# Split probabilities for the third block of the first batch, roundings on ScalarE alone, and a planner that holds DMAs back

## The chip, the cores and the metric

The kernel runs on one core of a Trainium2 chip. The metric is device microseconds of one execution. Times are compared between kernels run on the same chip.

## The reference

Two batches of 8 heads (768 tokens, head size 64) go through an attention whose mask joins only tokens with equal hash buckets; the result, as 1536 tokens of 512, goes through two gated layers of width 2048.

```python
def _attn_ref(q, k, v, proj):
    q_bits = (np.einsum('bhsd,dk->bhsk', q, proj) > 0).astype(np.int64)   # 6 hash bits, k likewise
    ...
    mask = q_bucket[:, :, :, None] == k_bucket[:, :, None, :]
    scores = scale * np.matmul(q, k.transpose(0, 1, 3, 2))
    scores = np.where(mask, scores, -1000000000.0)
    scores = scores - np.max(scores, axis=-1, keepdims=True)
    attn = np.exp(scores)
    attn = attn / (np.sum(attn, axis=-1, keepdims=True) + 1e-09)
    return np.matmul(attn, v)

def _moe_ref(x, w_in, w_out):        # _moe2_ref: g = h * clip(h + 3, 0, 6) / 6
    h = x @ w_in
    g = h * (1.0 / (1.0 + np.exp(-h)))
    return g @ w_out
```

The four weight matrices arrive as 64-bit floats, all else as 32-bit.

## The kernel before

**Stages.** A matrix product of nearly fp32 precision is made of three fp16 products: each operand is a high part (its rounding to fp16) and a low part (the rest). The work is, in program order: the preparation of four head pairs of batch 0 (load q and k, scale, split into high and low parts, transpose by DMA, hash, transpose again), their attention, the first layer of batch 0 (`mlp1`), the same for batch 1, then the second layer of both batches (`mlp2`).

**Attention.** A `Unit` is one head pair and one block of two query tiles; it has four slots (two tiles by two heads). Batch 0 has 4 pairs by 3 blocks, so 12 units and 48 slots, as has batch 1. A slot is: four score matmuls (L755, L756), a row maximum on VectorE (L759), two tiny steps (L761, L764), the exponential `e` on ScalarE (L767), and the product with v. That product comes in two kinds. An exact slot (`exact_values`) turns the fp32 `e` on TensorE (L783, six transposes), copies the result out of PSUM in two halves (L789), and multiplies in fp32 (L795, six matmuls that the trace shows as twelve). A split slot (`split_values`) rounds `e` to a high part `PN` (L814 on ScalarE or L815 on VectorE), subtracts for the low part (L816 on GpSimd or L817 on VectorE), has both turned by one DMA on SP's queue (L819), and multiplies in fp16 with the split `V` (L809, 18 matmuls). In the kernel before, all 48 slots of batch 0 are exact (`NX = 12`) and read v as it was loaded; all of batch 1 are split.

**Weights.** W1I and W1O are the two matrices of the first layer, in 16 chunks each. A chunk is loaded into one of three staging buffers `st` (L450); ScalarE or GpSimd makes a copy (L452, L453), GpSimd clears part of `st` (L455), and VectorE puts the bits together in two steps (L457, L459), the second of which frees the buffer. The scales come out of sums over all chunks of a matrix: W1O's scale needs all 16 of its chunks. Then each of the 32 pieces is split into a high and a low part. The first product of `mlp1` (L882) needs W1I; the second (L939, destination `h` from `G`) needs W1O. The second layer's matrices go the same way later.

**split().** The helper makes a high part on GpSimd (L392) or on ScalarE (L393), and a low part on VectorE (L400) from the source and the high part. It splits weights, the gated activations `G` of `mlp1`, `V` of batch 1, and q and k of each pair. Of q (i = 0) it uses another form (L385 to L390): GpSimd scales in place, ScalarE copies, GpSimd or VectorE subtracts.

**What sets the order.** No order is written out. `Plan` records every step with its engine, or with several engines to choose from, a cost in us, and what it reads and writes. `Run` then walks through the steps as a list scheduler: it takes at each point the step that can start first, ties by rank, and chooses among engines by the earlier end. VectorE steps marked `True` and all of GpSimd's are kept from running at the same time (`port`). 24 passes, forward and backward in turn, improve the ranks; the forward run with the shortest modelled length is kept, and the instructions of all engines are issued in its order. Each engine, and SP's queue of DMAs, then runs its instructions strictly in that order and waits where an operand isn't there.

## Time and profile before

| | |
|---|---|
| median of three runs | 773.67 us (772.26 to 777.58) |
| the profiled execution's own time | 777.89 us |
| its span in the trace | 776.2 us |
| instructions in the trace | 15453 |
| TensorE busy | 717.7 us (92%) |
| VectorE busy | 519.3 us (67%) |
| ScalarE busy | 460.1 us (59%) |
| GpSimd busy | 256.2 us (33%) |
| mean granted TensorE clock | 0.978 |

The span runs from the first to the last instruction; the execution's own time has 1.7 us around it. A share of busy time is a mean over stages with different limits, so the stretches are read apart. In the rows, PE is TensorE, PEld its weight loads, DVE VectorE, ACT ScalarE, POOL GpSimd, SPq SP's queue of DMAs.

### The profile page before, as it was taken

How to read it: one execution, taken by the hardware profiler on the slowest of the kernel's cores; microseconds unless marked ns; L12 is line 12 of the kernel's file. 1: busy time of each engine (PE TensorE's matmuls, PEld its weight loads, DVE VectorE, ACT ScalarE, POOL GpSimd, SP SyncE). 2: the span in 40 equal slices, each digit the busy share in tenths (PEclk: the TensorE clock that was granted, in tenths of full speed). 3: DMA queues.
4: the chain of work that ended last, by engine and by line, in shares of the span. 5: the costliest groups of instructions: out<-in, count | busy, mean ns of one | idle time of the engine just before them, and what ended most of it. 6: DMA issues, size and time to landing. Idle time of an engine off the chain costs nothing.

```text
span 776.2 us, 15453 instructions
## 1 busy us (share of the span) xinstructions
PE 717.7 (92%) x6012; PEld 535.7 (69%) x6012; DVE 519.3 (67%) x1147; ACT 460.1 (59%) x941; POOL 256.2 (33%) x263
## 2 busy tenths in 40 slices
PE   1498999999768999999989999999999999999997
PEld 1287898988647888887878888984444664444564
DVE  5798799898993876689777685879433343333343
ACT  6497799987633758888754646546333434323433
POOL 3435232444554546667734353521000000000000
PEclk9998899999988999999999999999999999999999
DMA  9999535759465478699953536000000100000100
GB/s 283 251 254 216 173 111 174 159 139 224 137 126 103 90 126 162 146 177 169 185 167 110 190 109 214 5 1 1 1 1 0 55 1 28 1 1 0 55 1 28
DMA packets 157385, 84.89 MB, mean 109 GB/s; under 512 B 139904, under 2 KB 147072, under 8 KB 157312
## 3 DMA queue, kind: packets, MB, share of 16 engines
q1 hardware_dynamic: 157312, 83.91, 44.6%
q8 instruction: 47, 0.77, 0.4%
q14 instruction: 26, 0.21, 0.1%
HBM read 44.57 MB, written 3.15 MB: 61 GB/s over the span
## 4 chain that ended last, share of the span: by engine, by line
PE 67%; DVE 11%; DMA 7%; ACT 6%; issue 3%; POOL 2%; SPq 0%; POOLq 0%; ACTq 0%; DVEq 0%
PE h L882 27%; PE s L1027 16%; PE h L939 10%; PE o L795 5%; PE s L755 3%; PE s L756 2%; DVE w L400 2%; PE h L783 2%; DVE nm L759 2%; PE o L809 2%; DMA st<-in_moe_w_in_dram 2%; ACT e L767 2%; DMA PT<-PN 2%; DMA st<-in_moe_w_out_dram 1%; DMA T<-N 1%
## 5 line engine op out<-in xcount | busy, mean ns | idle before, releaser
L939 PE MATMUL h<-G,w 128*128 128x256 f16 x1152 | 137.3, 277 | 4.2 <-DVE w L400 4.2
L1027 PE MATMUL s<-y,G 128*128 128x512 f16 x576 | 134.4, 379 | 0.8 <-ACT w L1043 0.8
L939 PEld LDWEIGHTS <-w 128*128 128x128 f16 x1152 | 112.7, 100 | 21.0 <-DVE w L400 5.3
L882 PEld LDWEIGHTS <-w 128*128 128x128 f16 x1152 | 112.6, 99 | 18.0 <-DVE g L927 1.8
L759 DVE TENSOR_REDUCE nm<-s 128x1 f32<-128x768 f32 x96 | 91.1, 952 | 25.0 <-PE s L756 24.4
L767 ACT ACTIVATE e<-s,nb,sc 128x768 f32<-128x768 f32 x96 | 95.0, 991 | 20.3 <-DVE nb L764 16.6
L1014 ACT ACTIVATE g<-h,table 128x256 f32<-128x256 f32 x96 | 50.7, 562 | 83.4 <-PE h L882 83.3
L1027 PEld LDWEIGHTS <-G 128*128 128x128 f16 x576 | 56.3, 98 | 62.8 <-issue 1.1
L816 POOL TENSOR_TENSOR PN<-e,PN 128x768 f16<-128x768 f32 x48 | 80.4, 1679 | 37.6 <-ACT PN L814 28.0
L1018 DVE TENSOR_SCALAR g<-g 128x512 f32<-128x512 f32 (+1 forms) x64 | 23.5, 367 | 94.5 <-ACT g L1014 94.5
L882 PEld LDWEIGHTS <-T 128*128 128x128 f16 x576 | 56.3, 98 | 42.2
L795 PE MATMUL o<-w,PT 128*128 128x64 f32 x576 | 72.4, 278 | 1.4 <-DVE x L844 1.4
L455 POOL TENSOR_SCALAR st<-st 128x512 f32<-128x512 f32 x64 | 46.1, 724 | 82.8 <-ACT w L452 34.7
L795 PEld LDWEIGHTS o<-w,PT 128*128 128x128 f32 x576 | 70.9, 198 | 2.6 <-DVE x L844 1.9
L755 PE MATMUL s<-T 128*128 128x384 f16 x192 | 65.5, 341 | 7.4 <-ACT e L767 7.3
L1021 ACT ACTIVATE G<-g 128x512 f16<-128x512 f32 (+1 forms) x64 | 33.4, 522 | 61.1 <-DVE g L1020 59.5
L882 PE MATMUL h<-X,w 128*128 128x256 f16 x576 | 67.7, 272 | 0.9 <-DVE g L927 0.9
L756 PE MATMUL s<-T 128*128 128x384 f16 x192 | 65.6, 342 | 3.0 <-DMA T<-N 2.8
L882 PE MATMUL h<-T,w 128*128 128x256 f16 x576 | 65.8, 276 | 2.0 <-DVE g L927 2.0
L1022 DVE TENSOR_TENSOR G<-g,G 128x512 f16<-128x512 f32 (+1 forms) x64 | 35.7, 558 | 39.2 <-ACT G L1021 38.5
L392 POOL TENSOR_SCALAR G<-g,table 128x512 f16<-128x512 f32 x39 | 43.1, 1105 | 40.2 <-DVE g L927 34.1
L882 PE MATMUL h<-X,T 128*128 128x512 f16 (+1 forms) x288 | 50.7, 326 | 0.0
(136 smaller groups left out, 1159.9 us busy)
## 6 DMA issues: line engine op xcount, KB each, us to landing
st<-in_moe_w_in_dram SPq DMA_DIRECT2D x32, 512.0 KB, 4.3
st<-in_moe_w_out_dram SPq DMA_DIRECT2D x32, 512.0 KB, 4.0
qk<-in_v_dram SPq DMA_DIRECT2D x8, 384.0 KB, 3.7
out_dram<-w SPq DMA_DIRECT2D x12, 256.0 KB, 2.0
qk<-in_q_dram SPq DMA_DIRECT2D x6, 384.0 KB, 3.4
qk<-in_k_dram SPq DMA_DIRECT2D x6, 384.0 KB, 4.0
w<-in_v_dram SPq DMA_DIRECT2D x2, 768.0 KB, 9.6
T<-T SPq DMA_DIRECT2D x8, 192.0 KB, 3.6
```

Of the source, the lines that this page charges most:

```text
L392: op([(POOL, Cost.pool_ts(n), lambda: nc.gpsimd.tensor_scalar(hi(), src(), scale(), 1.0, op0=ALU.mult, op1=ALU.mult)), (ACT, Cost.act_ap(n ...
L455: op((POOL, Cost.pool_ts(512), lambda: nc.gpsimd.tensor_scalar(st.t[:, :, 1].bitcast(F32), st.t[:, :, 1].bitcast(F32), 0.0, 1.0, op0=ALU.m ...
L755: nc.tensor.matmul(o, t.t[:, 0, c, :], t.t[:, 1, ks, :], start=True, stop=False)
L756: nc.tensor.matmul(o, t.t[:, 2, c, :], t.t[:, 3, ks, :], start=False, stop=True)
L759: op((DVE, 0.865, lambda: nc.vector.tensor_reduce(nm.t, ps.t[:, :, :HS], op=ALU.max, axis=AX.XY, negate=True)), [(ps, 0)], [(nm, 0)])
L767: op((ACT, 0.97, lambda: nc.scalar.activation(e.t.rearrange("p (n c) -> p n c", n=2), ps.t[:, :, :HS], AF.Exp, bias=nb.t, scale=sc.t, accu ...
L795: nc.tensor.matmul(po(), pt.t[:, kt, :], vraw.t[:, v0 + a, kt * D : (kt + 1) * D], start=(kt == 0), stop=(kt == T - 1))
L816: op(ways((POOL, Cost.pool_tt(S), lambda: nc.gpsimd.tensor_tensor(pn.t[:, 1], e.t, pn.t[:, 0], op=ALU.subtract)), (DVE, Cost.tt(S), lambda ...
L882: nc.tensor.matmul(ph, W[f, wl, kt, :], XT[b].t[:, kt, ts, xl, :], start=(c == 0), stop=(c == 3 * NK - 1))
L939: nc.tensor.matmul(pf.t[:, :n], W1O[f, wl, slice(m * P, (m + 1) * P)], G.t[:, f, gl], start=(f == 0 and c == 0), stop=(f == NF - 1 and c = ...
L1014: nc.scalar.activation(g.t[:, cs], pf.t[:, cs], AF.Relu, bias=three, scale=a)
L1027: nc.tensor.matmul(acc[m // 2].t[:, m % 2, :DM], gs.t[:, f % 3, gl, m * P : (m + 1) * P], W2O[f, wl], start=(f == 0 and c == 0), stop=(f = ...
```

## The change

Three edits, one of which sits in the planner, so that nearly the whole order of instructions is another.

**Which slots are exact.** `exact(p, blk)` takes the place of `NX`: blocks 0 and 1 of batch 0 stay exact (32 slots), block 2 (16 slots) becomes split. So v of batch 0 is split as well, four pieces of 768 elements per partition.

**Roundings.** `split()` makes every high part on ScalarE; the choice of GpSimd and the in-place form for q are gone, and so is GpSimd's choice for the copy of a weight chunk. Over the program this takes 39 high parts of weights, 39 of `G`, 5 + 2 of q and k, 3 of `V` and 4 chunk copies from GpSimd, and for the eight q splits the scaling in place and the subtraction; VectorE gets eight low parts more for q and four for `V`. By the program's lists GpSimd goes from 268 to 179 instructions, ScalarE from 742 to 817, VectorE from 1149 to 1159, and SP from 202 to 218 (16 more transposes of `PN`).

**The planner.** In the forward and backward runs a step of SP starts no earlier than 2.0 us (`QUEUE`) before the modelled end of the transfers already issued. This holds in the planner alone: on the chip SP waits for nothing more than before. What changes is the place of a DMA in the order.

```diff
@@ -40,6 +40,7 @@
 
     DMA_ISSUE, DMA_START = (0.51, 1.22), (1.1, 1.27)
     TURN_END = 0.86
+    QUEUE = 2.0
 
     WINDOW, WARM = 10240 / 3000, 1.294
 
@@ -127,7 +128,7 @@
         self.last = [[-10.0] * 5 for _ in ops]
         self.free, self.held, self.port = [0.0] * 5, {}, 0.0
         self.order, self.engines, self.ends = [], [None] * n, [0.0] * n
-        data, clock = 0.0, Clock(always=back)
+        self.data, clock = 0.0, Clock(always=back)
         self.pending = [[] for _ in range(5)]
         for i in range(n):
             if not left[i]:
@@ -140,7 +141,7 @@
             way = next(w for w in self.ways[i] if w[0] == e)
             time = way[1]
             if e == SP:
-                end = data = max(s + Cost.DMA_START[o.turn], data) + time
+                end = self.data = max(s + Cost.DMA_START[o.turn], self.data) + time
                 self.free[e] = max(s + Cost.DMA_ISSUE[o.turn], o.turn * (end - Cost.TURN_END))
             elif e == PE:
                 end = self.free[e] = clock.run(s, time)
@@ -171,6 +172,9 @@
         r = self.free[e]
         if e == POOL or e == DVE and shared(next(w for w in self.ways[i] if w[0] == e)):
             r = max(r, self.port)
+        if e == SP:
+
+            r = max(r, self.data - Cost.QUEUE)
         if self.take[i] is not None:
             held = self.held.get(self.take[i], 0.0)
             if held is None:
@@ -379,19 +383,9 @@
 
         op((ACT, Cost.act(n) + 0.093, fn), reads, writes)
 
-    def split(hi, lo, src, scale, n, reads, hi_cell, lo_cell, in_place=None, spare=True):
-
-        if in_place is not None:
-            op((POOL, Cost.pool_ts(n), lambda: nc.gpsimd.tensor_scalar(src(), src(), scale(), 1.0, op0=ALU.mult, op1=ALU.mult)),
-               reads, [in_place])
-            op((ACT, Cost.act(n), lambda: nc.scalar.activation(hi(), src(), AF.Copy)), [in_place], [hi_cell])
-            op([(POOL, Cost.pool_tt(n), lambda: nc.gpsimd.tensor_tensor(lo(), src(), hi(), op=ALU.subtract)),
-                (DVE, Cost.tt(n), lambda: nc.vector.tensor_tensor(lo(), src(), hi(), op=ALU.subtract), True)],
-               [in_place, hi_cell], [lo_cell])
-            return
-        op([(POOL, Cost.pool_ts(n), lambda: nc.gpsimd.tensor_scalar(hi(), src(), scale(), 1.0, op0=ALU.mult, op1=ALU.mult)),
-            (ACT, Cost.act_ap(n), lambda: nc.scalar.activation(hi(), src(), AF.Copy, scale=scale()))],
-           reads, [hi_cell])
+    def split(hi, lo, src, scale, n, reads, hi_cell, lo_cell, spare=True):
+
+        op((ACT, Cost.act_ap(n), lambda: nc.scalar.activation(hi(), src(), AF.Copy, scale=scale())), reads, [hi_cell])
 
         def pool_lo():
             nc.gpsimd.tensor_scalar(src(), src(), scale(), 1.0, op0=ALU.mult, op1=ALU.mult)
@@ -449,9 +443,7 @@
             sc = (st, 0)
             op((SP, Cost.load(512), lambda: nc.sync.dma_start(st.t.rearrange("p n w -> p (n w)"), src.bitcast(I32))),
                (), [sc])
-            op([(ACT, Cost.act(512), lambda: nc.scalar.activation(dst(), st.t[:, :, 1].bitcast(F32), AF.Copy, scale=TINY)),
-                (POOL, Cost.pool_ts(512), lambda: nc.gpsimd.tensor_scalar(
-                    dst(), st.t[:, :, 1].bitcast(F32), TINY, 1.0, op0=ALU.mult, op1=ALU.mult))], [sc], [cell])
+            op((ACT, Cost.act(512), lambda: nc.scalar.activation(dst(), st.t[:, :, 1].bitcast(F32), AF.Copy, scale=TINY)), [sc], [cell])
             op((POOL, Cost.pool_ts(512), lambda: nc.gpsimd.tensor_scalar(
                 st.t[:, :, 1].bitcast(F32), st.t[:, :, 1].bitcast(F32), 0.0, 1.0, op0=ALU.mult, op1=ALU.mult)), [sc, cell], [sc])
             op((DVE, 0.602, lambda: nc.vector.scalar_tensor_tensor(
@@ -654,7 +646,7 @@
                 hi = lambda i=i, c=c: N.t[:, i, :, c : c + D]
                 lo = lambda i=i, c=c: N.t[:, i, :, D - c : 2 * D - c]
                 split(hi, lo, r, lambda i=i: self.sc.t[:, i : i + 1], 2 * TD, [(self.raw, i), (self.sc, 0)],
-                      (N, i, i), (N, i, 1 - i), in_place=None if i else (self.raw, i))
+                      (N, i, i), (N, i, 1 - i))
 
         def turn(self, n):
             op((SP, Cost.turn(4 * T), lambda: nc.sync.dma_start_transpose(
@@ -708,13 +700,15 @@
         def values(self):
             h = 2 * self.hp
             if self.b == 0:
-
-                self.vraw = vall[h // HP], h % HP
-                return
+                r = vall[h // HP]
+                src = lambda: r.t[:, h % HP : h % HP + 2]
+                self.vraw = r, h % HP
+                if all(exact(self, blk) for blk in range(len(blocks[0]))):
+                    return
+            else:
+                r = v_pair(self.b, self.hp)
+                src = lambda: r.t
             V = self.V = buf(ep, f"V{self.n % 4}", [P, 2, 2, TD], F16)
-            r = v_pair(self.b, self.hp)
-            src = lambda: r.t
-            self.vraw = r, 0
             split(lambda: V.t[:, :, 0], lambda: V.t[:, :, 1], src, lambda: v_s[self.b], 2 * TD,
                   [(r, 0), ("v_s", self.b)], (V, 0), (V, 1), spare=False)
 
@@ -1047,7 +1041,11 @@
 
 
     NE, NPN, NPT = 2, 3, 3
-    NX = 12
+
+    def exact(p, blk):
+
+        return p.b == 0 and blk < 2
+
     wslots = [(wp, f"w{i}") for i in range(9)]
     prs = [Pair(n) for n in range(B * HP)]
     v_all()
@@ -1056,7 +1054,7 @@
         p.prepare()
         p.values()
     for n, (p, blk) in enumerate(units):
-        Unit(p, blk, n < NX)
+        Unit(p, blk, exact(p, blk))
     W1I = Weight("W1I", w1_in, True, wslots[0:4], [wslots[i] for i in (4, 0, 1, 2)], grouped=True)
     W1O = Weight("W1O", w1_out, False, [wslots[i] for i in (8, 7, 5, 6)], [wslots[i] for i in (3, 8, 7, 5)], after=W1I)
     for blk in range(len(blocks[0])):
```

VectorE's list where the last pieces of W1O are split (names `w`; in the kernel before the high parts of 10 of these 16 pieces are made by GpSimd). Before:

```order
L400 SCALAR_TENSOR_TENSOR w_2988<-w_1652,table,w_2988 128x512 x4
L400 SCALAR_TENSOR_TENSOR G<-g_2845,table,G 128x2x256
L679 TENSOR_REDUCE hs<-p_hash 128x72
L400 SCALAR_TENSOR_TENSOR w_3048<-w_2186,table,w_3048 128x512 x4
L400 SCALAR_TENSOR_TENSOR G<-g_2918,table,G 128x2x256
L400 SCALAR_TENSOR_TENSOR w_3081<-w_2496,table,w_3081 128x512 x4
L362 TENSOR_SCALAR hx<-p_tot 128x2
```

The same place now:

```order
L394 SCALAR_TENSOR_TENSOR w_2309<-w_1639,table,w_2309 128x512 x4
L755 TENSOR_SCALAR sc_2401<-nm_2326,table 128x1
L921 SCALAR_TENSOR_TENSOR g_2360<-g_2360,h_2287 128x512
L394 SCALAR_TENSOR_TENSOR V_2368<-qk,table,V_2368 128x2x384
L758 TENSOR_SCALAR nb_2423<-nm_2326,sc_2401 128x1
L394 SCALAR_TENSOR_TENSOR G<-g_2284,table,G 128x2x256
L394 SCALAR_TENSOR_TENSOR w_2405<-w_1816,table,w_2405 128x512 x2
L394 SCALAR_TENSOR_TENSOR G<-g_2360,table,G 128x2x256
L394 SCALAR_TENSOR_TENSOR w_2405<-w_1816,table,w_2405 128x512
L753 TENSOR_REDUCE nm_2489<-s_2279 128x1
```

The last low part of W1O was VectorE's 490th instruction and is now its 404th: 40 row maxima stand ahead of it where 55 did, since the units of block 2 moved behind it.

ScalarE's list at the same place (W1O's high parts; `e` is a slot's exponential, `PN` its high part, `sq` a sum of squares). Before:

```order
L814 ACTIVATE PN_2926<-e_2912 128x768
L393 ACTIVATE w_2988<-w_1652,table 128x512 x2
L378 ACTIVATE sq,qkss_3039<-qk 128x768
L393 ACTIVATE w_3048<-w_2186,table 128x512
L378 ACTIVATE sq,qkss_3039<-qk 128x768
L393 ACTIVATE w_3081<-w_2496,table 128x512 x2
```

And now:

```order
L382 ACTIVATE sq,xparts<-x_1650 128x256
L388 ACTIVATE w_2309<-w_1639,table 128x512 x4
L919 ACTIVATE g_2360<-h_2287,table 128x512
L388 ACTIVATE V_2368<-qk,table 128x2x384
L842 ACTIVATE xn<-x_2036 128x2x128
L388 ACTIVATE G<-g_2284,table 128x2x256
L388 ACTIVATE w_2405<-w_1816,table 128x512 x2
L388 ACTIVATE G<-g_2360,table 128x2x256
```

All four high parts of a group of pieces now stand in ScalarE's list, between the steps of `mlp1`.

SP's queue at the start (`qk` and the first `w` are q and k of the first two pairs, `w` from `v` the values of batch 0, `st` weight chunks). Before:

```order
L620 DMA w_106<-in_k_dram 128x2x384
L450 DMA st_109<-in_moe_w_in_dram 128x1024
L450 DMA st_114<-in_moe_w_in_dram 128x1024
L594 DMA w_116<-in_v_dram 128x4x384
L594 DMA w_118<-in_v_dram 128x4x384
L450 DMA st_122<-in_moe_w_in_dram 128x1024
L660 DMA_TRANSPOSE T_181<-N 128x24x128
```

And now:

```order
L612 DMA w_106<-in_k_dram 128x2x384
L586 DMA w_112<-in_v_dram 128x4x384
L444 DMA st_135<-in_moe_w_in_dram 128x1024
L444 DMA st_161<-in_moe_w_in_dram 128x1024
L586 DMA w_168<-in_v_dram 128x4x384
L652 DMA_TRANSPOSE T_189<-N 128x24x128
```

One weight chunk fewer stands ahead of the first pair's transpose; up to the last transpose of the fourth pair it is 8 chunks where there were 10.

## Rows read from the trace of the kernel before

**Rows 1.** The page's first line and its chain of work (part 4)

```profile
span 776.2 us, 15453 instructions
...
PE 67%; DVE 11%; DMA 7%; ACT 6%; issue 3%; POOL 2%; SPq 0%; POOLq 0%; ACTq 0%; DVEq 0%
...
```

**Rows 2.** Stretches: busy us of PE, PEld, DVE, ACT, POOL; clock; DMA

```profile
...
100.00:160.00 60.00, 59.15 (x518) 53.81 (x518) 56.52 (x148) 57.93 (x134) 23.95 (x30) 1.00 0.53 143
160.00:203.90 43.90, 42.51 (x413) 37.77 (x413) 39.53 (x86) 33.33 (x69) 18.91 (x21) 1.00 0.77 189
203.90:237.20 33.30, 21.24 (x174) 14.55 (x170) 32.48 (x55) 14.03 (x24) 19.69 (x18) 0.80 0.56 121
0.00:237.20 237.20, 188.93 (x1622) 162.47 (x1623) 203.75 (x491) 176.60 (x378) 102.09 (x124) 0.95 0.73 185
237.20:521.70 284.50, 279.16 (x3046) 241.76 (x3047) 207.29 (x433) 184.84 (x375) 150.31 (x134) 0.99 0.59 132
521.70:776.20 254.50, 249.60 (x1347) 131.51 (x1344) 108.24 (x224) 98.68 (x188) 3.85 (x5) 0.99 0.04 13
...
```

**Rows 3.** The chain in order of time, 0 to 265: start us, us, what

```profile
...
30.12 6.72 DMA st<-in_moe_w_in_dram
...
231.17 5.93 DVE w L400 x4
237.15 13.65 PE h L939 x107
...
```

**Rows 4.** The same chain: pieces of exact and of split slots

```profile
98.57 0.66 PE h L783 x6
...
99.23 1.29 PE o L795 x12
...
281.59 0.16 PE s L755
...
284.20 0.53 PE o L809 x18
```

**Rows 5.** VectorE groups by form: busy us, mean ns | idle before

```profile
...
L759 DVE TENSOR_REDUCE nm<-s 128x1 f32<-128x768 f32 x96 | 91.1, 952 | 25.0 <-PE s L756 24.4
...
L400 DVE SCALAR_TENSOR_TENSOR w<-w,table,w 128x512 f16<-128x512 f32 x32 | 28.5, 920 | 0.6 <-POOL w L392 0.6
...
L761 DVE TENSOR_SCALAR sc<-nm,table 128x1 f32<-128x1 f32 x96 | 19.6, 208 | 1.3
...
L400 DVE SCALAR_TENSOR_TENSOR y<-y,table,y 128x512 f16<-128x512 f32 x16 | 11.4, 745 | 0.0
...
L679 DVE TENSOR_REDUCE hs<-p_hash 128x72 f32<-128x504 f32 x16 | 10.8, 678 | 1.3 <-PE p_hash L673 1.0
...
L400 DVE SCALAR_TENSOR_TENSOR N<-qk,qksc,N 128x768 f16<-128x768 f32 x6 | 8.3, 1382 | 0.8 <-POOL N L392 0.8
...
L400 DVE SCALAR_TENSOR_TENSOR V<-qk,table,V 128x768 f16<-128x768 f32 x4 | 4.0, 1006 | 0.0
...
```

**Rows 6.** ScalarE and GpSimd groups of the same view

```profile
...
L767 ACT ACTIVATE e<-s,nb,sc 128x768 f32<-128x768 f32 x96 | 95.0, 991 | 20.3 <-DVE nb L764 16.6 <-POOL PN L816 2.2 <-PE p_tot L354 0.7
...
L789 ACT ACTIVATE PT<-h 128x384 f32<-128x384 f32 x96 | 42.8, 495 | 7.9 <-PE h L783 7.5
...
L392 POOL TENSOR_SCALAR w<-w,table 128x512 f16<-128x512 f32 x25 | 20.4, 827 | 15.0 <-DVE w L400 13.2 <-DVE table L368 1.5 <-DVE table L492 0.4
...
L393 ACT ACTIVATE w<-w,table 128x512 f16<-128x512 f32 x7 | 4.8, 716 | 6.0 <-DVE w L400 6.0
...
```

**Rows 7.** VectorE in time: the step ending chunks 16, 32, 38, 62

```profile
113.29 0.68 DVE L459 SCALAR_TENSOR_TENSOR w<-st,w 128x512 int32<-128x512 int32 x1
...
202.52 1.34 DVE L459 SCALAR_TENSOR_TENSOR w<-st,w 128x512 int32<-128x512 int32 x1
...
403.92 0.69 DVE L459 SCALAR_TENSOR_TENSOR T<-st,T 128x512 int32<-128x512 int32 x1
...
483.88 0.68 DVE L459 SCALAR_TENSOR_TENSOR y<-st,y 128x512 int32<-128x512 int32 x1
```

## The prediction

> **What bounds the kernel now.** I read the chain first, then busy time by stretches, then the chain in order of time, then the groups. TensorE has 67% of the chain of a span of 776.2 us, VectorE 11%, DMA 7% [rows 1]. The shares are not spread evenly. From 237.2 on TensorE is busy for 279.16 of 284.5 us and then for 249.60 of 254.5 [rows 2]: whatever TensorE is spared there comes off the end, and the last stretch has no edit in it. Up to 237.2 it is another kernel: TensorE is busy for 188.93 us, VectorE for 203.75, ScalarE for 176.60 [rows 2]. In 100 to 160 three engines are full together (59.15, 56.52 and 57.93 of 60), and in 203.9 to 237.2 VectorE alone is (32.48 of 33.3, TensorE 21.24). The chain shows what ends this stage: VectorE makes the last low parts of W1O up to 237.1, and from 237.15 TensorE runs 107 matmuls of L939 that waited for them [rows 3]. I call the end of that last low part **the mark**. The span is the mark, plus TensorE's work behind it, plus small losses. So the sum has three terms: where the mark goes, what TensorE has left behind it, and what it loses there.
>
> **TensorE's work.** An exact slot's transposes cost 0.66 us and its values 1.29, a split slot's values 0.53 [rows 4]. Each of 16 slots saves 0.66 + 1.29 - 0.53 = 1.42 us, together 22.7. The position matters more. By the program's order 48 exact slots, 55 score slots and 3 split slots stand ahead of the mark before; now 32, 40 and 6 do. That is 16 x 1.95 = 31.2, plus 15 x 4 x 0.16 = 9.6 for score matmuls [rows 4], less 3 x 0.53 = 1.6: 39 us, and 40 with a few hash products, leave the stretch ahead of the mark. Since only 22.7 of them vanish, TensorE has 17 us **more** to do behind it. An earlier mark must first pay for that.
>
> **The mark, by VectorE.** Ahead of it VectorE has 490 instructions before and 404 now, 86 fewer. 15 row maxima go with their two tiny steps: 15 x (0.952 + 2 x 0.208) = 20.5 us; 4 hash sums of 0.678 are 2.7 [rows 5]. About 42 short ones remain; at the 0.208 of the shortest row shown they would be 8.7, and I take 6, since records of short instructions overlap. Added are three more low parts of q and two of `V`: 1.006 for one on its own, 1.382 for the mean of `N` [rows 5], so 5.0 to 6.9; I take 5.5, nearer to the row without GpSimd beside it. The roundings that leave GpSimd add something else. A low part of 512 elements takes 0.745 us where nothing runs on GpSimd (`y`), and 0.920 in the mean for W1 (`w`) [rows 5]; over 32 pieces that is 5.6 us of waiting, and as GpSimd's high parts at 0.827 [rows 6] are gone but not its subtractions, I take half, 3, with 0 and 5.6 as ends. Sum: 203.75 - 20.5 - 2.7 - 6 + 5.5 - 3 = 177.
>
> The Trainium skill, in SBUF (Who interferes with whom), says that a VectorE instruction with two inputs in SBUF and a GpSimd instruction that reads SBUF exclude each other for a whole instruction, and that a reduction never waits. That speaks partly against this change, which puts 16 more subtractions of that kind on GpSimd; by the program's order two of them more lie ahead of the mark than before and the rest where VectorE has room, so by the rule the term of 3 would be nearer to 0 and the forecast 3 us later. The trace agrees so far as the 0.745 against 0.920 show it.
>
> **The mark, by ScalarE.** Ahead of the mark go 32 copies of turned probabilities at 0.495 (15.8) and 14 exponentials at 0.991 (13.9); 25 high parts of W1 and 7 of `G` come at about 0.716 (22.9) [rows 6]. The rest, more high parts of q and `V` against fewer copies and sums of squares, I estimate at +5 from the same rows (14 parts half as long again, less some twenty short steps). Net -2: 175 us of 176.60.
>
> So both engines have about 176 us to do, where VectorE alone had 204. VectorE was busy for 86% of the stretch up to the mark. With that share the mark comes at 177 / 0.86 = 206. Ends: 198 if the share rises to 0.895, half way to the 0.94 of 100 to 160 [rows 2]; 217 if two equally full queues that wait for each other give 0.81. The start is in this too: SP's queue has two weight chunks fewer ahead of the fourth pair's transposes, and a chunk stood in the chain at 30.12 with 6.72 us [rows 3], which bounds what the planner's rule gives between 0 and 6.7 us; I count none of it apart.
>
> **Behind the mark.** ScalarE had 184.84 us in 237.2 to 521.7. Over the program 39 + 39 high parts of weights and `G` come to it at 0.716, 56 us; 23 of them and 7 lay ahead of the mark, and the exponentials of block 2 now follow it: it comes to about 250 of 302, 83%. VectorE goes from 207.29 to about 235, GpSimd from 150.31 to fewer. TensorE loses 5.3 of 284.5 us there now [rows 2]; I add 3, from 0 to 10. The 16 new transposes of `PN` run beside a DMA share of 0.59 and cost nothing while TensorE has `mlp1` products to put between; without those each would show some us, as the chain's 7% of DMA do now [rows 1].
>
> **The sum.** 776.2 - (237 - 206) + 17 + 3 = 765 us of span; with the 1.7 us around it 767, against 777.89 of that execution: 0.986. Applied to the median of 773.67 this is **763 us**. Below I give times on the scale of the median. The break-even point is a mark at 237 - 17 - 3 = 217.
>
> **Rivals.**
> 1. *ScalarE takes VectorE's place; nothing comes of it.* It had slack at the end of the stage (14.03 of 33.3 us, and 33.33 of 43.9 [rows 2]), but now has W1O's high parts there. If up to 160 it gets through no more than before (about 129 us, the rows' 176.60 less 33.33 and 14.03) and then goes at the 0.76 of 160 to 203.9, the missing 46 us take 60: mark at 220, span 776.2 - 17 + 17 + 3 = 779, median 776. For it: 57.93 of 60 us in 100 to 160. Against: 40 us of TensorE work that paced just that stretch are gone. The Trainium skill, in Perfetto Trace Analysis (Optimizing Scalar/DVE Operations), advises moving work between those two engines when one of them is saturated; here both are in 100 to 160, so by that rule this rival would have more weight than I give it.
> 2. *A thinner TensorE runs slower.* In 203.9 to 237.2, with 21.24 of 33.3 us busy, its granted clock was 0.80 [rows 2]. About 32 us of its work stand between the last exact slot and the mark. If all of it ran at 1.2 instead of 2.4 GHz it would take 64 where some 56 are there: mark at 213, span 772, median 770. The Trainium skill, in Perfetto Trace Analysis (Matmul Optimizations), says that the engine scales power with utilization and that matmuls should follow each other; the 0.80 agrees.
> 3. *The staging buffers set the pace; slower.* Chunk 16 ends at 114.0 and chunk 32 at 203.9 [rows 7], 5.6 us a chunk, through three buffers that SP refills in order; now the lists want the same 16 chunks in about 55 us, 3.4 each. If the pace stays, the mark stays at 237 and only the 17 + 3 us are left: span 796, median 794. It decides from 217 - 33 = 184 for chunk 32, 4.4 us a chunk. For it: four engines and a DMA follow each other for every chunk, and two of those engines are fuller. Against: chunks 38 to 62 take (484.6 - 404.6) / 24 = 3.3 us each [rows 7].
> 4. *All 22.7 us come off.* The mark at 237 - 40 = 197 and no loss: span 776.2 - 40 + 17 = 753.5, median 751. It needs both engines at 0.9 from the first us on.
>
> That the change doesn't do what it says applies to the planner's rule alone: no instruction on the chip waits for it.
>
> **How the numbers follow.** The forecast has 0.47, rival 1 0.18, rival 2 0.07, rival 3 0.18, rival 4 0.10. A measurement of this kernel can tell about 1% from no change, 766 to 781. The forecast's own ends, marks at 198 to 217 with 0 to 10 us of loss, are 752 to 781; three quarters of it I put below 766. Faster: 0.10 of rival 4 and 0.35 of the forecast, 0.45. Same: rivals 1 and 2 but for a tail of 0.02, and the rest of the forecast, 0.35. Slower: rival 3 and that tail, 0.20. The range goes from rival 4 to nearly half way from rival 1 to rival 3: 750 to 784.
>
> **What would show it.** In the new profile the chain should leave VectorE's low parts of W1O for the second product of `mlp1` near 206, with VectorE and ScalarE both at 170 to 180 us busy by then and TensorE at about 150; from there to the start of `mlp2` TensorE should be busy for all but 8 us, and the last 254.5 us should be the same. The W1O chunks should end some 33 us ahead of the mark, near 172. If ScalarE is the releaser of most of VectorE's and TensorE's idle time ahead of the mark, it is rival 1; if SP's loads wait for L459's successor and both engines idle, rival 3; a clock under 0.8 between 150 and 206, rival 2. The prediction is wrong if the mark doesn't move by more than 20 us, or if TensorE idles for more than 15 us behind it.

## The result, and the profile after

The changed kernel took 747.26 us in the median of four runs (745.56 to 747.44), the kernel before 774.54 beside it (772.26 to 777.58): a ratio of 0.964, 95% interval 0.960 to 0.968. The time is 16 us under the forecast of 763 and below its range.

From the page of the changed kernel, the first line, busy times (part 1) and the chain (part 4):

```profile
span 745.7 us, 15542 instructions
...
PE 689.2 (92%) x6012; PEld 507.9 (68%) x6012; DVE 507.3 (68%) x1157; ACT 513.1 (69%) x1016; POOL 182.5 (24%) x174
...
PE 56%; DMA 13%; ACT 12%; DVE 10%; issue 5%; POOL 2%; SPq 2%; POOLq 0%; ACTq 0%; DVEq 0%
```

Against [rows 1] TensorE's share of the chain fell from 67% to 56%, while DMA's went from 7% to 13% and ScalarE's from 6% to 12%. The end of W1O's low parts, on VectorE in time:

```profile
178.66 2.73 DVE L394 SCALAR_TENSOR_TENSOR w<-w,table,w 128x512 f16<-128x512 f32 x4
...
183.74 1.41 DVE L394 SCALAR_TENSOR_TENSOR w<-w,table,w 128x512 f16<-128x512 f32 x2
...
185.73 0.74 DVE L394 SCALAR_TENSOR_TENSOR w<-w,table,w 128x512 f16<-128x512 f32 x1
...
188.03 0.74 DVE L394 SCALAR_TENSOR_TENSOR w<-w,table,w 128x512 f16<-128x512 f32 x1
```

The mark is at 188.8, where it was at 237.1 [rows 3]. The stretches, with the columns of [rows 2]:

```profile
100.00:160.00 60.00, 45.24 (x351) 37.62 (x348) 55.30 (x130) 57.76 (x115) 18.79 (x20) 0.87 0.63 189
160.00:174.00 14.00, 13.60 (x165) 11.56 (x165) 13.71 (x27) 13.34 (x25) 5.15 (x4) 0.83 0.80 168
174.00:188.80 14.80, 14.48 (x163) 12.46 (x161) 14.80 (x27) 14.17 (x28) 5.38 (x4) 1.00 0.41 105
0.00:188.80 188.80, 144.27 (x1272) 122.21 (x1272) 166.66 (x404) 170.20 (x343) 47.86 (x63) 0.95 0.77 203
188.80:491.20 302.40, 294.79 (x3389) 253.73 (x3390) 243.93 (x548) 249.83 (x495) 134.66 (x112) 1.00 0.74 164
491.20:745.70 254.50, 250.16 (x1353) 131.96 (x1351) 96.67 (x206) 93.05 (x179) 0.00 (x0) 1.00 0.04 13
```

The 30.5 us of span add up in two ways. By stretches: the mark 48.4 earlier, the stretch behind it 17.9 longer (284.5 to 302.4), the last 254.5 the same. By TensorE: 717.7 to 689.2 us busy, and 58.5 to 56.5 idle (span less busy). By the second way 28.5 us of TensorE's time went, and no waiting came in their place.

Not all of the 28.5 us is removed work, because matmuls take longer at a lower clock: 24 value matmuls of exact slots took 5.01 us at 74.86 in the kernel before, where the granted clock was 0.50, and 2.63 at 84.66, where it was 1.00. It was 0.50, the lower of its two levels (1.2 GHz), in four stretches before (73.6 to 83.8, 210.1 to 220.3, 234.0 to 240.8 and 397.8 to 401.3, here as their sum) and in one now:

```profile
sum 30.70, PE 24.95 PEld 17.73 DVE 22.04 ACT 15.15 POOL 12.97; mean PE 6.24 PEld 4.43 DVE 5.51 ACT 3.79 POOL 3.24
```

```profile
144.20:164.60 20.40, 10.83 (x54) 6.39 (x54) 17.70 (x43) 18.39 (x37) 8.58 (x7) 0.50 0.70 180
```

Half of the busy time in these stretches, 12.5 us before and 5.4 now, is an estimate, from these rows, of what the lower clock cost. So some 7 of the 28.5 us are clock, and some 21.4 are removed work, for the 22.7 of the prediction. Reckoned in this way, TensorE's work is 681 to 687 us in every kernel below that has the split third block, and 704 to 708 in every one that hasn't.

The chain of work runs differently as well. In the kernel before it went from the last low part of W1O straight to the second product [rows 3]. In the changed kernel, in order of time:

```profile
168.84 0.66 DVE w L394
...
171.44 4.83 issue
...
183.83 4.55 DMA qk<-in_k_dram
...
189.84 1.33 PE h L933 x12
```

The last low parts, up to 188.8, are not in it. TensorE no longer waits for the mark itself: with the first groups of W1O ready it is busy for 14.48 of the last 14.8 us ahead of it. The mark is still the time by which the work of this stage is done, but it is not what releases TensorE.

### The profile page after: what moved, and what is told of

Its sections match the earlier page's. It is cut to its first block, busy times and chain, and to the rows that moved or that the text cites. A ratio compares the mean times of both kernels' runs of the same rounds, so it can differ in the third digit from the quotient of the medians.

```text
span 745.7 us, 15542 instructions
## 1 busy us (share of the span) xinstructions
PE 689.2 (92%) x6012; PEld 507.9 (68%) x6012; DVE 507.3 (68%) x1157; ACT 513.1 (69%) x1016; POOL 182.5 (24%) x174
## 4 chain that ended last, share of the span: by engine, by line
PE 56%; DMA 13%; ACT 12%; DVE 10%; issue 5%; POOL 2%; SPq 2%; POOLq 0%; ACTq 0%; DVEq 0%
PE h L876 22%; PE s L1021 17%; PE h L933 9%; DMA T<-G 3%; DMA PT<-PN 3%; ACT e L761 3%; ACT sq L382 3%; PE o L789 2%; DVE nm L753 2%; DMA st<-in_moe_w_in_dram 2%; PE s L749 2%; PE s L750 2%; PE o L803 1%; PE h L777 1%; ACT PN L808 1%
## 5 line engine op out<-in xcount | busy, mean ns | idle before, releaser
L933 PE MATMUL h<-G,w 128*128 128x256 f16 x1152 | 134.1, 273 | 0.1
L810 POOL TENSOR_TENSOR PN<-e,PN 128x768 f16<-128x768 f32 x64 | 107.8, 1687 | 73.5 <-ACT PN L808 55.3
L876 PEld LDWEIGHTS <-w 128*128 128x128 f16 x1152 | 112.0, 99 | 20.0 <-issue 2.7
L933 PEld LDWEIGHTS <-w 128*128 128x128 f16 x1152 | 110.7, 98 | 14.3 <-issue 0.5
L1008 ACT ACTIVATE g<-h,table 128x256 f32<-128x256 f32 x96 | 50.6, 561 | 88.0 <-PE h L876 87.9
L1021 PEld LDWEIGHTS <-G 128*128 128x128 f16 x576 | 56.2, 98 | 62.7 <-issue 1.1
L753 DVE TENSOR_REDUCE nm<-s 128x1 f32<-128x768 f32 x96 | 91.2, 951 | 11.1 <-PE s L750 10.4
L447 POOL TENSOR_SCALAR st<-st 128x512 f32<-128x512 f32 x64 | 50.3, 787 | 140.3 <-ACT w L446 59.8
L876 PE MATMUL h<-X,w 128*128 128x256 f16 x576 | 71.8, 276 | 1.1 <-DVE g L921 1.1
L808 ACT ACTIVATE PN<-e 128x768 f16<-128x768 f32 x61 | 51.1, 840 | 6.8 <-DMA PT<-PN 6.5
L876 PE MATMUL h<-T,T 128*128 128x512 f16 (+1 forms) x288 | 50.7, 326 | 0.0
L789 PE MATMUL o<-w,PT 128*128 128x64 f32 x384 | 46.2, 271 | 0.2 <-DVE x L838 0.2
```

The costliest lines, as they stand in the source:

```text
L447: op((POOL, Cost.pool_ts(512), lambda: nc.gpsimd.tensor_scalar(st.t[:, :, 1].bitcast(F32), st.t[:, :, 1].bitcast(F32), 0.0, 1.0, op0=ALU.m ...
L753: op((DVE, 0.865, lambda: nc.vector.tensor_reduce(nm.t, ps.t[:, :, :HS], op=ALU.max, axis=AX.XY, negate=True)), [(ps, 0)], [(nm, 0)])
L789: nc.tensor.matmul(po(), pt.t[:, kt, :], vraw.t[:, v0 + a, kt * D : (kt + 1) * D], start=(kt == 0), stop=(kt == T - 1))
L808: op(ways((ACT, Cost.act(S), lambda: nc.scalar.activation(pn.t[:, 0], e.t, AF.Copy)), (DVE, 0.47, lambda: nc.vector.tensor_copy(pn.t[:, 0] ...
L810: op(ways((POOL, Cost.pool_tt(S), lambda: nc.gpsimd.tensor_tensor(pn.t[:, 1], e.t, pn.t[:, 0], op=ALU.subtract)), (DVE, Cost.tt(S), lambda ...
L876: nc.tensor.matmul(ph, W[f, wl, kt, :], XT[b].t[:, kt, ts, xl, :], start=(c == 0), stop=(c == 3 * NK - 1))
```

## The experiments

The edits are called S (the split third block), A (the roundings on ScalarE alone) and Q (the planner's rule). Each row is one kernel with one list of instructions. Mark, busy times ahead of it, the mean of W1's low parts on VectorE and TensorE's times are read from its profile; TensorE's idle time is the span less its busy time. In e15 GpSimd makes one of the 32 low parts, and the mean is over 31. Ratios are to the kernel before on the same chip, with 95% intervals.

| kernel | edits | ratio | mark | VectorE, ScalarE busy ahead | low part, ns | TensorE busy, idle |
|---|---|---|---|---|---|---|
| before | none | 1 | 237.1 | 203.7, 176.6 | 920 | 717.7, 58.5 |
| e3 | Q | 0.990 (0.985 to 0.994) | 232.1 | 202.7, 179.1 | 979 | 711.0, 55.3 |
| e1 | S | 0.986 (0.983 to 0.989) | 204.3 | 184.3, 165.0 | 948 | 696.0, 71.3 |
| e6 | S, Q | 1.000 (0.997 to 1.004) | 204.1 | 182.6, 161.9 | 917 | 693.8, 78.8 |
| e2 | A | 0.975 (0.972 to 0.977) | 217.6 | 186.1, 195.8 | 812 | 708.7, 47.9 |
| e5 | A, Q | 0.974 (0.970 to 0.979) | 210.8 | 178.7, 189.1 | 745 | 706.4, 50.6 |
| e17 | A, Q at 1.8 | 0.975 (0.971 to 0.979) | 212.6 | 180.5, 189.8 | 744 | 708.2, 49.0 |
| e4 | S, A | 0.979 (0.977 to 0.982) | 202.8 | 175.3, 176.5 | 843 | 697.9, 67.2 |
| e14 | S, A, other list | 0.979 (0.975 to 0.983) | 201.5 | 176.5, 177.1 | 809 | 693.9, 67.3 |
| e15 | S, A, third list | 0.967 (0.963 to 0.971) | 175.9 | 154.1, 159.4 | 787 | 691.5, 61.4 |
| e7 | S, A, Q at 1.0 | 0.970 (0.966 to 0.974) | 202.0 | 173.9, 176.7 | 843 | 693.8, 60.8 |
| e16 | S, A, Q at 1.6 | 0.962 (0.958 to 0.966) | 190.5 | 168.0, 171.6 | 786 | 687.9, 56.8 |
| e11 | S, A, Q at 1.8 | 0.975 (0.971 to 0.980) | 193.8 | 171.1, 173.4 | 862 | 690.5, 64.0 |
| after | S, A, Q at 2.0 | 0.964 (0.960 to 0.968) | 188.8 | 166.7, 170.2 | 756 | 689.2, 56.5 |
| e12 | S, A, Q at 2.2 | 0.968 (0.963 to 0.974) | 193.9 | 174.3, 174.6 | 788 | 690.4, 55.0 |
| e8 | S, A, Q at 4.0 | 0.975 (0.971 to 0.980) | 209.3 | 185.7, 186.0 | 886 | 694.8, 65.8 |
| e9 | after's list, high parts on GpSimd | 0.977 (0.972 to 0.982) | 204.7 | 179.3, 154.5 | 1010 | 697.8, 63.0 |
| e10 | list before, high parts on ScalarE | 1.002 (1.000 to 1.005) | 236.4 | 196.8, 201.9 | 825 | 714.6, 62.7 |

### The parts one by one

`e1_split_alone` has S in the kernel before; so that the products of one PSUM group stay in their order, two dependencies are written out.

```diff
-    NX = 12
+    def exact(p, blk):
+        return p.b == 0 and blk < 2
...
-        Unit(p, blk, n < NX)
+        Unit(p, blk, exact(p, blk))
...
-                           gc + W1O.cells(f) + W1O.cells(f + 1), [(pf, f)]))
+                           gc + W1O.cells(f) + W1O.cells(f + 1) + ([(pf, f - 2)] if f else []), [(pf, f)]))
```

> The kernel before with the third block of the first batch split, and nothing else of the change (two order dependencies that the planner's order had kept by itself are written out). Three theories. A, the shared port: what the forecast missed is VectorE waiting for GpSimd, which goes only when the roundings leave GpSimd, and ScalarE has room for them only when the copies of exact slots are gone; the two edits need each other and the queue rule gives little. Then this alone leaves VectorE's waits: VectorE about 180 us busy ahead of the end of W1O's low parts, that mark at about 209, some 17 to 20 us more for TensorE behind it, in all 1% faster (764 to 768). B, a sum of parts: each edit gives its own share whatever the others do, and this one gives TensorE's 22.7 us (750 to 754). C, the queue rule: it makes the better start and keeps engines fed, and half of the 27 us are its own; this alone gives 762 to 768.

`e2_scalar_alone` has A in the kernel before.

```diff
-        op([(POOL, Cost.pool_ts(n), lambda: nc.gpsimd.tensor_scalar(hi(), src(), scale(), 1.0, op0=ALU.mult, op1=ALU.mult)),
-            (ACT, Cost.act_ap(n), lambda: nc.scalar.activation(hi(), src(), AF.Copy, scale=scale()))],
-           reads, [hi_cell])
+        op((ACT, Cost.act_ap(n), lambda: nc.scalar.activation(hi(), src(), AF.Copy, scale=scale())), reads, [hi_cell])
```

> The kernel before with all high parts and chunk copies on ScalarE, and nothing else of the change. A: VectorE loses some 13 us of waiting ahead of the mark, but ScalarE gains about 40 us there on 176.6 and becomes the bound: mark between 230 and 245, time within 1% (767 to 781). B: 5 to 10 us faster (764 to 769). C: no change (770 to 778).

`e3_queue_alone` adds Q to the kernel before, and `e4_without_queue` takes it out of the changed one:

```diff
+        if e == SP:
+            r = max(r, self.data - Cost.QUEUE)
```

> The kernel before with the planner's queue rule, and nothing else of the change. A: 0 to 7 us faster by an earlier fourth pair (767 to 774). B: about 3 us faster (771). C: 10 us faster or more (764 or less), with the first 100 us clearly fuller.

> The changed kernel without the queue rule: split third block and roundings on ScalarE. A: 747 to 752, mark at 185 to 190 and VectorE's low parts of W1 at about 0.76 us each. B: 750. C: 757 or more, with the loss in the first 100 us.

S alone gave 1.4%, A alone 2.5%, Q alone 1.0%; S with A gave 2.1%, less than A alone. e1 (766.9 us, mark 204.3) is inside the ranges of theories A and C, and B's 750 to 754 fell. e2, at 758.6 us, is faster than all three theories had it, so the theory that S and A need each other fell with it. e3, at 768.1, is inside A and outside C. e4, at 762.1, is outside A and B, which ends the plain sum of parts; C had it there, but C fell with e3. The other two pairs:

`e5_without_split` is the changed kernel with `return p.b == 0` in `exact`; `e6_without_scalar` has the old `split()` and chunk copies put back in it.

```diff
-        return p.b == 0 and blk < 2
+        return p.b == 0
```

> The roundings and the planner's rule without the split third block (edits 2 and 3); all 48 slots of batch 0 exact. Roundings alone gave 758.6 us with a mark at 217.6. Theory R (the queue rule is worth something of its own, about 14 us at the mark and 6 behind it, as between the changed kernel and the one without the rule): mark near 205, 742 to 750 us. Theory L (the rule only draws another list out of the planner, and lists of one kind scatter by about 1%): mark 210 to 222, 752 to 766 us. Theory S (the rule pays only where the third block's transposes of PN crowd the queue): 756 to 760 us, mark 215 to 218.

> The split third block and the planner's rule without the roundings on ScalarE (edits 1 and 3). Split alone gave 766.9 us, mark 204.3, TensorE idle 14.8 us behind it. The shared-port theory: VectorE keeps some 184 us ahead of the mark, so the mark stays above 198 and the time above 757. Theory R: the rule takes about 14 off the mark and 6 off the idle time, 747 to 752 us, without the roundings. Theory L: 755 to 770 us.

e5 (759.3 us, mark 210.8) is outside theory R, inside L, and has S's time but not its mark. e6 (778.6 us, mark 204.1, VectorE 182.6) is as the shared-port theory stated, and slower than R and L had it. Q brought nothing to A, and with S it took S's gain away, each time with one list. Each kernel planned with A has a lower ratio than each planned without it. TensorE's columns show how the parts work together. S takes 11 to 22 us off TensorE's busy time, a scatter that comes mostly from the clock, but it adds idle time: 12.8 and 23.5 us without A (58.5 to 71.3, and with Q 55.3 to 78.8), and 4 to 19 with it (47.9 to 50.6 without S, 55.0 to 67.3 with it). A takes idle time off: 10.6 us in the kernel before (58.5 to 47.9), 4.7 beside Q (55.3 to 50.6), 4.1 beside S (71.3 to 67.2), 22.3 beside S and Q (78.8 to 56.5).

### One list, another engine

Here nothing is planned anew: the list of the kernel stays word for word, and only the engine that carries out the high parts is another, so that no new draw of the planner is in it. In `e9_high_parts_on_gpsimd` the 32 high parts of W1 go back to GpSimd:

```diff
-        op((ACT, Cost.act_ap(n), lambda: nc.scalar.activation(hi(), src(), AF.Copy, scale=scale())), reads, [hi_cell])
+        w1 = swap[0]
+
+        def high():
+            if w1:
+                nc.gpsimd.tensor_scalar(hi(), src(), scale(), 1.0, op0=ALU.mult, op1=ALU.mult)
+            else:
+                nc.scalar.activation(hi(), src(), AF.Copy, scale=scale())
+
+        op((ACT, Cost.act_ap(n), high), reads, [hi_cell])
```

> The changed kernel's own list of instructions, not planned anew, with the 32 high parts of W1I and W1O issued to GpSimd in place of ScalarE at the same places. The shared-port theory (a good part of the gain is that VectorE's low parts no longer wait for GpSimd): the low parts of W1 go from 757 ns back to 880 to 950, VectorE's busy time ahead of the mark from 167 to 171 to 176 us, the mark from 188.8 to 193 to 200, 751 to 758 us. The ScalarE theory (ScalarE, busy for 170 of 188.8 us ahead of the mark, sets it): it sheds some 23 us there, so the mark stays or comes earlier, 742 to 748 us.

VectorE's groups by form ahead of the mark, in the changed kernel:

```profile
L753 DVE TENSOR_REDUCE nm<-s 128x1 f32<-128x768 f32 x40 | 38.1, 952 | 3.9 <-PE s L750 3.6
...
L451 DVE SCALAR_TENSOR_TENSOR w<-st,w 128x512 int32<-128x512 int32 x32 | 23.4, 731 | 0.1
L394 DVE SCALAR_TENSOR_TENSOR w<-w,table,w 128x512 f16<-128x512 f32 x32 | 23.4, 756 | 0.0
...
L394 DVE SCALAR_TENSOR_TENSOR G<-g,table,G 128x512 f16<-128x512 f32 x8 | 6.2, 775 | 0.1
L394 DVE SCALAR_TENSOR_TENSOR N<-qk,qksc,N 128x768 f16<-128x768 f32 x6 | 6.0, 1007 | 0.0
```

and in e9:

```profile
L764 DVE TENSOR_REDUCE nm<-s 128x1 f32<-128x768 f32 x40 | 38.0, 950 | 4.3 <-PE s L761 4.2
L402 DVE SCALAR_TENSOR_TENSOR w<-w,table,w 128x512 f16<-128x512 f32 x32 | 31.6, 1010 | 1.1 <-POOL w L392 1.1
L460 DVE SCALAR_TENSOR_TENSOR w<-st,w 128x512 int32<-128x512 int32 x32 | 24.8, 775 | 0.1
...
L402 DVE SCALAR_TENSOR_TENSOR G<-g,table,G 128x512 f16<-128x512 f32 x8 | 7.9, 1003 | 0.0
```

The same 404 instructions keep VectorE busy for 179.28 us instead of 166.66: the low parts of W1 take 8.2 us more, those of `G` 1.7, the last chunk step 1.4. The row maxima, which read PSUM and reduce, take 950 ns with or without. ScalarE sheds 15.7 us (170.2 to 154.5), and yet the mark comes 15.9 us later and the span is 15.1 us longer. (The profiled execution of e9 is the slowest of its four; by the ratios, 0.977 against 0.964, the difference is 1.3%, some 10 us.) Of the mark's 15.9 us VectorE is busy for 12.6; the other 3.3 are idle time, 1.1 of it waiting for high parts that GpSimd makes in 967 ns where ScalarE took 739. So the shared-port theory holds in its direction and the ScalarE theory falls. All four sizes lie beyond the upper ends stated for it (950 ns, 176, 200 and 758 us; measured 1010, 179.3, 204.7 and 759.2): the port's cost was still taken too low.

`e10_before_high_parts_on_scalar` does the reverse in the list of the kernel before:

```diff
-        op([(POOL, Cost.pool_ts(n), lambda: nc.gpsimd.tensor_scalar(hi(), src(), scale(), 1.0, op0=ALU.mult, op1=ALU.mult)),
+        op([(POOL, Cost.pool_ts(n), lambda: nc.scalar.activation(hi(), src(), AF.Copy, scale=scale())),
```

> The list of the kernel before, not planned anew, with every high part that it gives to GpSimd (weights, G, V, k) issued to ScalarE at the same place; the in-place form for q and GpSimd's chunk copies stay. The shared-port theory: the low parts of W1 fall from 920 ns to about 750 to 780, VectorE is spared 8 to 14 us ahead of the mark, mark 222 to 231, ratio 0.980 to 0.993. The re-planning theory (the roundings' 2.5% come from what the planner can do with a freer GpSimd and other places, not from the durations): ratio 0.995 to 1.01, as ScalarE, at the old places, delays as much as VectorE gains.

Its stretches, as in [rows 2]:

```profile
0.00:236.40 236.40, 186.03 (x1621) 159.16 (x1621) 196.75 (x490) 201.87 (x419) 67.20 (x83) 0.99 0.73 188
236.40:522.80 286.40, 278.43 (x3041) 241.17 (x3042) 200.86 (x432) 209.46 (x415) 109.26 (x92) 0.99 0.57 130
```

VectorE is spared 7 us (203.7 to 196.75), ScalarE gets 25 more and is now the busier of the two, the mark stays. The low parts (825 ns) and the mark miss what the shared-port theory stated; the ratio is where the re-planning theory had it. At the old places these roundings are worth nothing. That the planner's new order makes the 2.5% of e2 fits this but is not shown, because e2 also takes the in-place form for q and four chunk copies from GpSimd, which e10 leaves there. ScalarE takes VectorE's place and nothing comes of it: that is what rival 1 of the prediction described, in a neighbouring kernel.

### How far lists scatter

Small changes of the rule: `QUEUE` at 1.0 (`e7_queue_one`), 4.0 (`e8_queue_four`), 1.8 (`e11_queue_less_a_little`), 2.2 (`e12_queue_more_a_little`), 1.6 with 60 passes (`e16_queue_1p6`), as

```diff
-    QUEUE = 2.0
+    QUEUE = 1.8
```

> The changed kernel with QUEUE 1.0 in place of 2.0. Theory R: a queue held shorter does nearly the same, 743 to 752 us, mark 184 to 194. Theory L: anywhere in 745 to 766 us, as likely near the 762.1 without the rule as near 747.3; mark and idle time behind it move apart from each other.

> The changed kernel with QUEUE 4.0 in place of 2.0, that is nearly one chunk of 512 KB more ahead in the queue. Theory R: between the changed kernel and the one without the rule, 747 to 757 us, in order of the rule's strictness (1.0, 2.0, 4.0, none). Theory L: anywhere in 745 to 766 us and out of that order.

> The changed kernel with QUEUE 1.8 in place of 2.0, a neutral change of the same rule. Theory R (the rule makes the 19 us between the changed kernel and the one without it): within 5 us of 747, ratio 0.959 to 0.970, mark 185 to 194. Theory L (lists that the planner draws scatter, and the one at 2.0 is a good one): ratio 0.968 to 0.985, mark 194 to 210.

> The changed kernel with QUEUE 2.2 in place of 2.0. The same two theories: R, ratio 0.959 to 0.970 and mark 185 to 194; L, ratio 0.968 to 0.985, mark 194 to 210, and not the same as with 1.8.

> The changed kernel with QUEUE 1.6 and 60 passes of the planner in place of 2.0 and 24: one more list with all three edits, which the planner itself holds for as short as that of the changed kernel. If what the changed kernel's list has ahead of the others is that W1O's last low parts meet no GpSimd step (0.74 us each, VectorE busy for all of the last 14.8 us ahead of the mark), this list is as fast only where its low parts are as short: at a mean of 750 to 770 ns a mark of 186 to 194 and a ratio of 0.960 to 0.968, at 800 to 850 ns a mark of 195 to 206 and 0.968 to 0.980.

The ratios, in order of strictness (1.0, 1.6, 1.8, 2.0, 2.2, 4.0), are 0.970, 0.962, 0.975, 0.964, 0.968 and 0.975: no order. The neighbour at 1.8 is slower; the one at 2.2 is not clearly so, as its interval overlaps. So theory R fell with e7, e8 and e11's ratio. e16 decides nothing: its low parts, at 786 ns, lie between the two cases that were stated for it. Without the rule, two neutral changes of a cost in the plan (5 ns on a form of GpSimd, on one of VectorE), the changed kernel again, and a second list without S:

```diff
-    pool_ts = staticmethod(lambda n: 0.245 + 0.00083 * n)
+    pool_ts = staticmethod(lambda n: 0.25 + 0.00083 * n)
```

> The changed kernel itself once more, beside the next three on one chip. Both theories: ratio 0.960 to 0.970, 745 to 752 us. If it scatters over 1% from execution to execution as the list at 2.2 did, part of the differences between lists is that of executions.

> Edits 1 and 2 without the planner's rule, with GpSimd's one-input steps costed 5 ns higher in the plan: a neutral change that gives another list. Theory R (the rule is worth most of the 1.6% between the changed kernel and the one without it): ratio 0.975 to 0.985 again. Theory L (the scatter of lists): anywhere in 0.962 to 0.985; a ratio under 0.970 would show that lists as good are had without the rule.

> The same with VectorE's two-input steps costed 5 ns higher in the plan, a third list without the rule. R: 0.975 to 0.985. L: anywhere in 0.962 to 0.985.

> Edits 2 and 3 with QUEUE 1.8 in place of 2.0, a second list without the split third block (the first gave 0.9744). If the split is worth what the sum of the prediction gave it (its mark earlier by some 20 us against 17 more behind), 0.972 to 0.980, and the mean of the lists with the split, 0.971, stays below both. If the split is worth nothing, 0.963 to 0.985, with no order between the two kinds.

The changed kernel came again at 0.962 (0.956 to 0.967), so a list repeats; e15 came to 0.967 without the rule, so lists nearly as good are had without it. e14 (0.979) and e17 (0.975) lie where both theories had them. Nine lists with S and A lie between 0.962 and 0.979, with or without Q: their mean is 0.971, that of the three without Q 0.975, of the six with it 0.969. Lists of A without S gave 0.974 to 0.975 three times. So Q's own worth (0.6% by these means) and S's beside A (0.4%) stay inside the scatter; that A makes most of the gain does not.

Of the nine lists, the four whose low parts average 788 ns or less have 0.962 to 0.968, the five at 809 or more 0.970 to 0.979. The end of e4 shows what low parts can meet, VectorE and then GpSimd in time:

```profile
186.67 2.79 DVE L391 SCALAR_TENSOR_TENSOR w<-w,table,w 128x512 f16<-128x512 f32 x2
...
189.57 1.42 DVE L365 TENSOR_SCALAR hx<-hx 128x2 int32<-128x2 int32 x1
...
199.62 3.20 DVE L391 SCALAR_TENSOR_TENSOR w<-w,table,w 128x512 f16<-128x512 f32 x2
```

```profile
186.84 4.12 POOL L807 TENSOR_TENSOR PN<-e,PN 128x768 f16<-128x768 f32 x2 [3.19 <-ACT PN L805]
...
200.19 2.08 POOL L807 TENSOR_TENSOR PN<-e,PN 128x768 f16<-128x768 f32 x1
```

Two low parts that take 1.41 us in the clear (above, at 183.74) take 2.79 and 3.20 beside GpSimd's subtractions for the split slots. In the changed kernel four take 2.73 (above). But this does not explain why the changed kernel is faster. Low parts of W1 and `G` and the two chunk steps together, 104 instructions ahead of the mark, keep VectorE busy for 77.2 us in the changed kernel, 78.3 in e4 and 76.3 in e14, which are two of the slowest lists. What e4 and e14 have more of is other work ahead of the mark, 424 and 420 VectorE instructions for 404, and more of TensorE's time at the lower clock (34 and 31 us of the span ahead of its end for 20). Why the changed kernel's list is one of the best stays open.

No list was clearly faster than the changed kernel; e16 (746.76 us) equals it.

## Why the prediction was wrong

**The step that failed** is the term of 3 us for waiting at the shared port, "half, 3, with 0 and 5.6 as ends", in the mark by VectorE. Ahead of the mark VectorE's busy time fell from 203.7 to 166.7 us where 177 was forecast. By forms, the row maxima with their tiny steps went from 74.3 to 54.6 (forecast -20.5, measured -19.7), hash sums -2.7 (as forecast), the rest by difference, short steps above all, -6.7 (forecast -6). The whole miss is in steps with two inputs: low parts of W1 28.5 to 23.4, of `G` 8.6 to 6.2, the two chunk steps 49.3 to 47.6, together -9.2 for the forecast's -3; and low parts of q, k and `V`, ten for 13.7 before, are fifteen for 15.0, +1.3 for the forecast's +5.5. That is 10.4 us more than forecast. e9 undoes it: with 12.6 us back on VectorE its mark is at 204.7, where the forecast had 206. Nor is the miss one of this list alone. The 104 low parts of W1 and `G` and chunk steps ahead of the mark keep VectorE busy for 84.7 to 87.8 us in the four kernels planned without A (86.4 before), for 73.3 to 79.6 in the twelve planned with it (77.2 in the changed kernel; e15 has 103 of the steps), for 78.9 in e10 and for 88.4 in e9. The error was to bound the port's cost by one group of low parts, where nearly all groups of steps with two inputs had been paying, the `N` at 1455 ns ahead of the mark before against 1007 now among them. `V` had not been (1006 and 1009 ns for the same form), nor had L921, one of whose inputs, `h`, is in PSUM (683 and 679). A freer port alone gives no time: in e10 VectorE is spared 7 us and the mark stays, with 25 us more on ScalarE.

The Trainium skill's rule in SBUF (Who interferes with whom) names the right instructions, and e9 agrees with it, 756 against 1010 ns beside a reduction that stays at 950 to 952. The conclusion drawn from it in the prediction, that the term is nearer to 0, was wrong: it counted the subtractions that the change adds to GpSimd and not the readers that it takes away.

**The path** came out otherwise too. The prediction had the chain leave VectorE's low parts of W1O for the second product of `mlp1`; it leaves them 19 us ahead of the mark (above).

**The share.** VectorE was busy for 166.7 of 188.8 us, 0.883, where 0.86 was assumed; 0.895 was the upper end. Of the 17 us between the mark of 206 and that of 188.8, 12 come from the 10.4 us (at 0.86), the rest from the share.

**What held.** ScalarE has 170.2 us ahead of the mark for the forecast's 175, and 249.8 of 302.4 behind it for the 250 of 302. TensorE's work behind the mark grew by 15.6 us (279.16 to 294.79) for the forecast's 17, and it idles there for 7.6 of 302.4 us, where 8 were allowed. The last 254.5 us are unchanged. So the sum holds for this list: with the mark at 206 in place of 188.8 the measured 745.7 would be 763, near the forecast's 765, and in e9 a mark 15.9 us later goes with a span 15.1 longer. It does not hold from list to list: from the mark to the end the nine lists with S and A take between 551 and 577 us, and the earliest mark, 175.9 in e15, does not give the shortest span. Three figures of the working are slightly off and change nothing: half way from 0.86 to 0.94 is 0.90, 177 / 0.81 is 218.5, and 776.2 - 40 + 17 is 753.2.

**What had no term.** The sum took the planner's list as given by the edits. Nine lists with S and A lie 1.7% apart, some 13 us, and the changed kernel's is one of the two best. e4, which has the two edits that the sum was made of, came to a span of 765.1 with its mark at 202.8, and to 762.1 us in the median for the forecast's 763. That agreement is luck: its two-input steps fell nearly as far as the changed kernel's, 20 more VectorE instructions stand ahead of its mark, which brings VectorE to 175.3 us near the forecast's 177, and its neighbour e15 came to 752.9. Q was counted at nothing, and no steady worth of it was found: -1.0% on the kernel before, none beside A, +1.4% beside S.

**The rivals.** Rival 4 (a mark at 197, 751 us, "both engines at 0.9") is what came nearest in the time: 0.883 and 0.90 (170.2 of 188.8). Its reason is not what made the time, since the mark came early mostly by VectorE's shorter busy time; the fuller engines gave 5 of the 17 us, and no run shows why they were fuller (in e9, with the port taken, VectorE still has 0.876). Rival 3 is refuted. Of the chunks' last step on VectorE:

```profile
99.65 0.79 DVE L451 SCALAR_TENSOR_TENSOR w<-st,w 128x512 int32<-128x512 int32 x1
...
152.24 1.67 DVE L451 SCALAR_TENSOR_TENSOR w<-st,w 128x512 int32<-128x512 int32 x1
```

Chunk 16 ends at 100.4 and chunk 32 at 153.9, 3.3 us a chunk; so the 5.6 of before [rows 7] were not the buffers' pace. Rival 2's condition came in part (a clock of 0.87 in 100 to 160 and 0.83 in 160 to 174; 0.50 from 144.2 to 164.6), its cost did not: TensorE is busy for only 144.27 of the 188.8 us, and VectorE and ScalarE for 55.30 and 57.76 of the 60. Rival 1's sign came by half. Of TensorE's 44.5 idle us ahead of the mark ScalarE ended 29 (exponentials and sums of squares above all), before 22 of 48.2; of VectorE's 22.1 it ended 2.4. So ScalarE is what TensorE waits for most in this stage, but it does not hold the mark: e9 spares it 15.7 us and the mark comes later.

## What to carry to other kernels

Before moving work off GpSimd, price it by every VectorE step with two inputs in the stage, each mean against the shortest of its form, and not by the mean of one group. Where the engine that takes the work is itself near full, the time counts only if the order changes too (e10). Where a list scheduler makes the order, an edit's time is a draw from lists that here lay 1.7% apart: measure a few neutral variations before crediting an edit with 1%, and keep the engine apart from the order by changing one in a fixed list. TensorE's busy and idle time, added up apart, show whether work that was removed has come back as waiting, once the time at the lower clock is taken out of the busy time.

## What the runs showed of the hardware that was not expected

A VectorE step with one input and two elements per partition can wait a whole GpSimd instruction too. In e9, VectorE and GpSimd in time:

```profile
164.11 0.17 DVE L372 TENSOR_SCALAR qksc<-hx 128x2 int32<-128x2 int32 x1
164.19 1.61 DVE L372 TENSOR_SCALAR inv<-hx 128x2 int32<-128x2 int32 x1
```

```profile
164.11 1.66 POOL L821 TENSOR_TENSOR PN<-e,PN 128x768 f16<-128x768 f32 x1
```

The step of 0.16 us (its mean in the changed kernel) takes 1.61, to within 0.03 us of the end of the subtraction that began just before it; the 1.42 us of L365 in e4 is another, ending at 190.99 where GpSimd's subtractions end at 190.96. And executions of one list need not agree: those of e12 went from 747.1 to 755.1 us, those of the changed kernel, with its repeat, from 745.6 to 750.0.
